# Splitting the last but one V chunk's load into three, and storing 48 rows instead of 128, in a one-core decode block

## The chip, the cores and the metric

The kernel runs on one core of one Trainium2 chip. The metric is the device time of one execution in microseconds (us). A core has five engines that work side by side and meet only at semaphores: PE (matmuls, with its weight loads shown as PEld), DVE and ACT (elementwise work), POOL (constants here) and SP (here it does nothing but issue transfers). The data of a transfer is moved by 16 DMA engines, which all work on the same transfer, each on some of its rows.

## The reference

One decode step: layer norm of a row `x` of 512, 32 query heads over 8 cached KV heads of 65536 keys each, the output projection, a residual, and a bilinear GLU with a second residual. Everything is float32.

```python
h  = x + A(layernorm(x))                    # A: the attention
h2 = h + B(layernorm(h))                    # B: (h Wgate * h Wup) Wdown
# A: q = (x @ wq) -> 32 heads of 128;  k_cache, v_cache: 8 heads x 65536 x 128
scores = einsum("bhqd,bhkd->bhqk", q, k) * 128 ** -0.5
p = softmax(scores);  o = einsum("bhqk,bhkd->bhqd", p, v);  return o @ wo
```

The caches are 512 MB of the 565 MB that are read; the rest is weights.

## The kernel before

The caches are cut into 64 chunks of 128 rows by 16384 columns of float32 (8 MB each): for each of the 8 heads four K chunks and then four V chunks, in the order in which they are used. Two tiles, `kv0` and `kv1`, take the even and the odd chunks in turn. SP issues every load, in a fixed order written out by hand (`even`, `odd`, a loop over the heads, and then the last loads one by one); before each load it waits for `free`, which DVE raises when PE is done with the tile's previous content. All loads stand in one queue, and the DMA engines work through it in order.

Chunk 62 is the last but one V chunk (of the last head) and the last that `even` loads. Behind it in the queue come chunk 63 in four pieces, the gate and up weights (`in_gu`) into `kv0`, the down weights (`in_wd`) into `kv1`, and at the very end the store of the result.

PE multiplies a chunk in 32 windows of 512 columns (`windows`, L365 of the profile). For an even chunk it waits for `s_k0` before window 0, for `s_k16` before 16, for `s_k24` before 24 and for `s_k28` before 28; each wait is for 16, and the amount is taken off again. A whole chunk is one load and raises only `s_k0`; so POOL puts 16 on the other three at the start for each even chunk (`sem_inc(p, w * (end // 2 + n))`, `end // 2` being 32). Only the weights `in_gu`, which come in four pieces, raise all four semaphores by themselves.

A transfer's own end is told by small packets: each DMA engine that took part writes one to the semaphore behind its data, 16 in all for a transfer of 128 rows.

At the end `pva` holds the result in two rows, 0 and 32, of 256 columns. DVE copies 64 rows of it into the tile `y` (128 by 256, set to zero at the start), SP stores the tile, and the host picks rows 0 and 32.

Of the kernel before, what the change touches and what calls it, by code (L numbers as in the profile page):

```python
# [3 lines left out]
F32 = mybir.dt.float32  # L4
# [4 lines left out]
P = 128  # L9
D = 512  # L10
HKV, REP, DH = 8, 4, 128
SK = 65536
CK = 16384
# [10 lines left out]
SIDE = 9  # L24
LATE = 1
WIDE = 384
DVE_ACT = bass.OrderedEngineSet([mybir.EngineType.DVE, mybir.EngineType.Activation])
K_CUTS = (0, 4, 8, 12, 16, 32)
V_CUTS = (0, 8, 12, 16, 24, 28, 32)
# [14 lines left out]
def body(nc, xr, kvd, wq0, wqo, wo7, gu, wd, out):  # L44
    pe_e, dve_e, act_e, pool_e, sp = nc.tensor, nc.vector, nc.scalar, nc.gpsimd, nc.sync

    def tile(name, *shape, align=32):
        return nc.alloc_sbuf_tensor(name, list(shape), F32, align_bytes=align).ap()
# [14 lines left out]
    kv = [tile(f"kv{i}", P, CK, align=1024) for i in range(2)]  # L63
# [3 lines left out]
    ln_s, ln_m, ln_v, ln_t, ln_r = (tile(n, 1, 1) for n in ("ln_s", "ln_m", "ln_v", "ln_t", "ln_r"))  # L67
    ln_w, ln_r3 = tile("ln_w", P, WIDE), tile("ln_r3", P, 1)
    ln_s3 = ln_w[:, 0:1]
# [9 lines left out]
    gu_sb, uf, y = tile("gu_sb", P, 512), tile("uf", P, 2, 2, 4, 2), tile("y", P, 256)  # L79
# [8 lines left out]
    def sem(name):  # L88
        sems.append(nc.alloc_semaphore(name))
        return sems[-1]  # L90
# [7 lines left out]
    s_k0, s_k16, s_k24, s_k28 = (sem(f"s_k{i}") for i in (0, 16, 24, 28))  # L98
    s_v0, s_v8, s_v16, s_v24, s_v28 = (sem(f"s_v{i}") for i in (0, 8, 16, 24, 28))
# [3 lines left out]
    late, s_act, s_pool, s_y, s_a, s_out = (sem(n) for n in ("late", "s_act", "s_pool", "s_y", "s_a", "s_out"))  # L103
    gu_t = kv[0].rearrange("p (k x) -> p k x", k=KT)[:, :, 0:2 * F]
    wd_t = kv[1]
    end = 2 * HKV * NT

    def take(e, s, n=1):
        e.wait_ge(s, n).then_inc(s, -n)  # L109
# [7 lines left out]
    def even(g):  # L117
        sp.dma_start(kv[0], kvd[g]).then_inc(s_k0, 16)

    def odd(g):  # L120
# [11 lines left out]
        out=ident, in_=ident, compare_op=ALU.not_equal, fill=1.0, base=0,  # L132
        pattern=[[-1, P]], channel_multiplier=1))
    pool.tick(pool_e.memset(qx, 0.0))
    for p, w, n in ((s_k16, 16, 0), (s_k24, 16, 0), (s_k28, 16, 0), (s_v8, 17, 0),
                    (s_v16, 16, -1), (s_v24, 16, -1), (s_v28, 16, -1)):
        pool_e.sem_inc(p, w * (end // 2 + n))
    for t in (o_pad, f_pad, sel_pad, acc, y, ln_w):
# [16 lines left out]
    take(sp, wf)  # L155
    sp.dma_start(wo_sb, wo7).then_inc(s_w, 16)
    take(sp, free)
    even(end - 2)
    take(sp, free)
    for lo, hi, p in ((0, 16, s_v0), (16, 24, s_v16), (24, 28, s_v24), (28, 32, s_v28)):  # L160
        cs = slice(lo * 512, hi * 512)
# [11 lines left out]
    for c in range(SIDE, NC):  # L173
# [13 lines left out]
        out=ln_m, in0=ln_s, scalar1=1.0 / D, scalar2=None, op0=ALU.mult))  # L187
    mine(dve_e.tensor_scalar(
        out=xd, in0=x_row, scalar1=ln_m[:, 0:1], scalar2=None, op0=ALU.subtract))
    dve_e.scalar_tensor_tensor(  # L190
        out=xs, in0=xd, scalar=1.0, in1=xd, op0=ALU.mult, op1=ALU.mult,
# [5 lines left out]
        out=xn_row, in0=xd, scalar1=ln_r[:, 0:1], scalar2=None, op0=ALU.mult).then_inc(dt, 1)  # L197
    dve_e.tensor_reduce(
        out=sel_h, in_=ident.rearrange("p (g h) -> p h g", h=REP), axis=AX.X, op=ALU.add).then_inc(own, 1)
# [4 lines left out]
        out=neg_mean, in0=mean_m, scalar1=sel_1[:, 0:1], scalar2=-1.0, op0=ALU.mult,  # L204
# [9 lines left out]
    qd = qx.rearrange("p (j x) -> p j x", j=4)  # L214
    with nc.Fori(0, HKV, engines=DVE_ACT):
        for s in range(NT):
# [20 lines left out]
        for s in range(NT):  # L237
# [12 lines left out]
            out=mrow, in_=sm[1][0:1, 0:P].rearrange("p (g h) -> p h g", h=REP), axis=AX.X,  # L250
# [5 lines left out]
            out=nbias, in0=sm[0][:, 0:1], scalar1=-SCALE, scalar2=None, op0=ALU.mult).then_inc(da, 1)  # L256
        for n in range(NT):
# [8 lines left out]
            if n == NT - 1:  # L266
                mine(dve_e.tensor_reduce(out=l1, in_=sums, axis=AX.X, op=ALU.add))
                dve_e.tensor_scalar(
                    out=l4, in0=sel_h, scalar1=l1[:, 0:1], scalar2=None, op0=ALU.mult).then_inc(tok, 1)
# [7 lines left out]
            else:  # L277
                for cs in (slice(0, 256), slice(256, 512)):
                    dve_e.tensor_tensor(  # L279
                        out=orow[:, cs], in0=ps[1][:, cs], in1=orow[:, cs], op=ALU.add).then_inc(tob, 1)  # L280
# [7 lines left out]
        for half, p in ((0, tok), (1, s_a)):  # L288
            cs = slice(half * 256, half * 256 + 256)
            dve_e.scalar_tensor_tensor(  # L290
                out=acc[:, cs], in0=attn[:, cs], scalar=1.0, in1=acc[:, cs], op0=ALU.mult, op1=ALU.add,
# [8 lines left out]
        out=acol, in_=ptp[1].rearrange("p (k j x) -> p k j x", k=KT, j=4)[:, :, :, 0], axis=AX.X,  # L300
# [4 lines left out]
    def centred(o, a):  # L305
# [8 lines left out]
        out=ln_q2, in0=hn, scalar=1.0, in1=hn, op0=ALU.mult, op1=ALU.mult,  # L314
        accum_out=ln_s3))
    dve_e.tensor_scalar(
        out=ln_s3, in0=ln_s3, scalar1=KT * EPS, scalar2=None, op0=ALU.add).then_inc(tl, 1)
    take(dve_e, kd)
    for half in range(2):
        cs = slice(half * 256, half * 256 + 256)  # L320
# [6 lines left out]
        out=sj[:, 0:2, :], in0=gux[0][:, :, :, 0], in1=uf[:, 0, :, :, 1], op=ALU.mult).then_inc(qt, 1)  # L327
# [4 lines left out]
        out=sj[:, 2, :], in0=gux[1][:, 0, :, 0], in1=uf[:, 1, 0, :, 1], op=ALU.mult)  # L332
    for o, g, u in ((f_pad[:, 0:1, 0], gux[0][:, 0, 3:4, 0], uf[:, 0, 1, 3:4, 0]),
# [3 lines left out]
            out=o, in0=g, scalar=ln_r3[:, 0:1], in1=u, op0=ALU.mult, op1=ALU.mult)  # L337
    i.then_inc(s_v8, 1)
    take(dve_e, kd)
    for half in range(2):  # L340
        cs = slice(half * 256, half * 256 + 256)
        dve_e.scalar_tensor_tensor(
            out=res[:, cs], in0=ps[1][:, cs], scalar=ln_r3[:, 0:1], in1=acc[:, cs],
# [37 lines left out]
    def step():  # L381
        pe_e.wait_ge(tl, next(once))
# [40 lines left out]
    step()  # L423
    mm(sm[0][:, 0:WIDE], mean_m, ln_w, start=True, stop=True).then_inc(pd, 1)
    for half in range(2):
# [64 lines left out]
    dve_e.tensor_copy(y[0:64, :], pva[0:64, 0:256]).then_inc(s_y, 1)  # L490
    take(sp, s_pool)
    sp.wait_ge(s_y, 1)
    sp.dma_start(out, y).then_inc(s_out, 16)
    nums = [s.num for s in sems]
    assert s_out.num == max(nums)
    sp.sem_clear(range(min(nums), s_out.num))
# [43 lines left out]
```

## Time and profile before

| What | Value |
|---|---|
| Median of 3 runs (lowest to highest) | 1309.93 us (1309.9 to 1310.06) |
| The profiled execution's own time | 1309.89 us |
| Its span, first to last instruction | 1308.5 us |
| Read from memory, over the span | 564.66 MB, 432 GB/s |
| Busy: PE, DVE, ACT | 52%, 9%, 4% of the span |
| DMA queue of SP | 99.8% of what 16 DMA engines have in time |

The profile is of one execution. The busy shares tell how long an engine worked, not whether anyone waited for it; that is read from the waits and from the chain of work that ended last. The DMA view can be asked for any stretch of the span: it then counts the packets that started in it, with their size classes, and the time that they took as a share of what 16 engines would have. The packets under 512 B are the semaphore packets.

### The profile page before, as it was taken

Reading aid. Unit: us, or ns where it says so; the run is one execution under the profiler, and the core shown is the slowest. Engines: PE = TensorE matmul, PEld = TensorE weight load, DVE = VectorE, ACT = ScalarE, POOL = GpSimd, SP = SyncE. Lnnn points to the kernel's source line nnn. Section 1 sums busy time; section 2 is a strip of 40 time slices with the busy share of each in tenths; the row PEclk is TensorE's granted clock in tenths of the full one; section 3 lists DMA queues with packets and bytes.
Section 4 is the critical chain, followed back from the end, with each engine's and each line's share of the span. In section 5 each row is a group of like instructions: output and inputs, shape, how many; then the busy total and the mean of one; then the engine's idle time right before and its main releaser. Section 6 shows DMA issues by size and latency. Waiting matters only on the chain. (4 is left out here: it accounts for less than half of the span.)

```text
span 1308.5 us, 10829 instructions
## 1 busy us (share of the span) xinstructions
PE 680.3 (52%) x4608; PEld 190.5 (15%) x4608; DVE 111.5 (9%) x286; ACT 54.9 (4%) x106; POOL 3.1 (0%) x13
## 2 busy tenths in 40 slices
PE   4355374454654545563554636535465445545466
PEld 1011111111111111111111111101111111111122
DVE  1000010100101001000010101001010010100101
ACT  0000000000000000000000000000000000000000
POOL 0000000000000000000000000000000000000000
PEclk8777786776867768767787767777687677886679
DMA  9999999999999999999999999999999999999998
GB/s 417 417 447 437 431 447 419 447 419 447 419 447 419 447 431 437 445 421 447 419 447 419 447 419 447 431 437 445 421 447 419 447 416 450 419 447 429 437 420 371
DMA packets 12931, 564.81 MB, mean 432 GB/s; under 512 B 1409, under 2 KB 1537, under 8 KB 2690
## 3 DMA queue, kind: packets, MB, share of 16 engines
q1 hardware_dynamic: 12928, 564.79, 99.8%
q8 instruction: 1, 0.02, 0.0%
q10 hardware_dynamic: 2, 0.00, 0.0%
HBM read 564.66 MB, written 0.13 MB: 432 GB/s over the span
## 5 line engine op out<-in xcount | busy, mean ns | idle before, releaser
L365 PE MATMUL ps<-kv,st 128*32 128x512 f32 x4184 | 584.2, 720 | 541.5 <-DMA kv<-in_kv 527.0
L365 PEld LDWEIGHTS ps<-kv,st 128*32 128x32 f32 x4184 | 145.1, 130 | 963.6 <-DMA kv<-in_kv 579.2
L244 DVE TENSOR_REDUCE mx<-sc 128x1 f32<-128x512 f32 x32 | 21.9, 686 | 538.0 <-DVEq L109 538.0
L415 PE MATMUL ptp<-ident,ex 128*128 128x128 f32 x128 | 27.9, 380 | 19.8 <-ACT ex L222 19.5
L218 ACT COPY sc<-ps 128x512 f32<-128x512 f32 x32 | 18.8, 586 | 451.1 <-ACTq L109 451.0
L276 DVE TENSOR_TENSOR orow<-ps,orow 128x512 f32<-128x512 f32 x16 | 11.1, 692 | 299.5 <-DVEq L109 299.5
L222 ACT ACTIVATE ex<-sc,nbias 128x512 f32<-128x512 f32 x32 | 22.8, 714 | 304.3 <-ACTq L109 304.3
L394 PE MATMUL ptp<-wqo_sb,xn 128*1 128x512 f32 x64 | 31.3, 636 | 6.4 <-DVE acc L290 5.0
L218 ACT ACT_TABLE_LOAD x8 | 10.3, 1283 | 436.3 <-ACTq L109 436.3
L263 DVE COPY st<-ptp 128x512 f32<-128x512 f32 x32 | 22.1, 692 | 44.9 <-DVEq L109 44.9
L415 PEld LDWEIGHTS ptp<-ident,ex 128*128 128x128 f32 x128 | 20.8, 193 | 22.7 <-ACT ex L222 22.6
L408 PE MATMUL sm<-ident,m 128*1 128x128 f32 x16 | 4.4, 276 | 27.2 <-DVE m L246 17.6
L279 DVE TENSOR_TENSOR orow<-ps,orow 128x256 f32<-128x256 f32 x16 | 6.0, 419 | 128.5 <-DVEq L109 128.5
L274 DVE COPY orow<-ps 128x512 f32<-128x512 f32 x8 | 5.5, 692 | 98.8 <-DVEq L109 98.8
L461 PE MATMUL attn<-wqo_sb,o_pad 128*32 128x512 f32 x64 | 8.5, 605 | 5.9 <-DVE o_pad L286 5.9
L410 PE MATMUL sm<-ones,mexp 1*128 1x1 f32 x32 | 6.9, 281 | 6.7 <-DVE mexp L253 6.7
L394 PEld LDWEIGHTS ptp<-wqo_sb,xn 128*1 128x1 f32 x64 | 5.0, 87 | 31.7 <-issue 18.9
L226 DVE COPY qrow<-ptp 1x512 f32<-1x512 f32 x8 | 5.4, 679 | 30.6 <-DVEq L109 30.6
L457 PE MATMUL ptp<-ident,orow 128*128 128x128 f32 x32 | 6.1, 300 | 3.0 <-DVE orow L279 3.0
L408 PEld LDWEIGHTS sm<-ident,m 128*1 128x1 f32 x16 | 1.3, 79 | 41.8 <-DVE m L246 24.9
L290 DVE SCALAR_TENSOR_TENSOR acc<-attn,acc 128x256 f32<-128x256 f32 x16 | 6.2, 422 | 10.8 <-DVEq L109 10.8
L398 PE MATMUL sm<-ident,qrow 1*128 1x1 f32 x32 | 3.2, 201 | 7.1 <-DVE qrow L226 7.1
(83 smaller groups left out, 78.0 us busy)
## 6 DMA issues: line engine op xcount, KB each, us to landing
wqo_sb<-in_wqo SPq DMA_DIRECT2D x7, 2048.0 KB, 32.7
kv<-in_kv SPq DMA_DIRECT2D x1, 4096.0 KB, 21.6
kv<-in_gu SPq DMA_DIRECT2D x1, 3584.0 KB, 18.8
kv<-in_kv SPq DMA_DIRECT2D x1, 2048.0 KB, 26.1
kv<-in_kv SPq DMA_DIRECT2D x2, 1024.0 KB, 29.1
kv<-in_gu SPq DMA_DIRECT2D x1, 1792.0 KB, 22.6
kv<-in_wd SPq DMA_DIRECT2D x1, 1536.0 KB, 19.3
kv<-in_wd SPq DMA_DIRECT2D x5, 256.0 KB, 20.9
```

The lines of the kernel that those rows point to most:

```text
L218: act_e.copy(sc[s], ps[s % 2]).then_inc(ad, 1)
L222: act_e.activation(ex[s - n], sc[s], AF.Exp, bias=nbias[:, 0:1], scale=SCALE, accum_out=sums[:, s:s + 1]).then_inc(atok[s - n], 1)
L244: dve_e.tensor_reduce(out=mx[:, s:s + 1], in_=sc[s], axis=AX.X, op=ALU.max).then_inc(own, 1)
L263: dve_e.tensor_copy(st[:, :, 0:16].rearrange("p g (b h) -> p b g h", h=REP), ptp[n % 2].rearrange("p (b g h) -> p b g h", b=4, h=REP)).the ...
L276: mine(dve_e.tensor_tensor(out=orow, in0=ps[n % 2], in1=orow, op=ALU.add))
L290: dve_e.scalar_tensor_tensor(out=acc[:, cs], in0=attn[:, cs], scalar=1.0, in1=acc[:, cs], op0=ALU.mult, op1=ALU.add, accum_out=rsum[:, hal ...
L365: i = mm(ps[buf][32 * j:32 * j + 32, :], st[:, 8 * j + r, :], kv[buf][:, w * 512:(w + 1) * 512], start=(r == 0), stop=(r in (2, 3, 7)), sk ...
L394: i = mm(ptp[0][0:1, :], xn[:, k:k + 1], wq_sb[:, k, :], start=(k == 0), stop=(k == KT - 1))
L410: mm(sm[0][:, 0:1], mexp.rearrange("p g h -> p (g h)"), ones[0:1, 0:1], start=True, stop=True).then_inc(pd, 1)
L415: i = pe_e.transpose(ptp[half][:, b * P:(b + 1) * P], ex[half][:, b * P:(b + 1) * P], ident)
L457: i = pe_e.transpose(ptp[1][:, b * P:(b + 1) * P], orow[:, b * P:(b + 1) * P], ident)
L461: i = mm(attn[32 * r:32 * r + 32, :], o_pad[:, r, :], wo_sb[:, r, :], start=True, stop=True)
```

## The change

Three things are edited.

1. SP loads chunk 62 in three transfers instead of one: columns 0 to 15487 of all 128 rows (raises `s_k0`), columns 15488 to 16383 (`SHARE`, 896 of them) of rows 0 to 119 (raises `s_k24`), and the same columns of rows 120 to 127 (raises `s_k28`).
2. POOL puts on `s_k24` and `s_k28` 16 less at the start, since chunk 62 raises them now by its own transfers.
3. The result's tensor has 48 rows instead of 128, and the store takes 48 rows of `y`; rows 0 and 32 are among them.

```diff
+SHARE = 896
...
-    for p, w, n in ((s_k16, 16, 0), (s_k24, 16, 0), (s_k28, 16, 0), (s_v8, 17, 0),
+    for p, w, n in ((s_k16, 16, 0), (s_k24, 16, -1), (s_k28, 16, -1), (s_v8, 17, 0),
                     (s_v16, 16, -1), (s_v24, 16, -1), (s_v28, 16, -1)):
         pool_e.sem_inc(p, w * (end // 2 + n))
...
-    even(end - 2)
+    for rows, cs, p in ((slice(0, P), slice(0, CK - SHARE), s_k0), (slice(0, 120), slice(CK - SHARE, CK), s_k24),
+                        (slice(120, P), slice(CK - SHARE, CK), s_k28)):
+        sp.dma_start(kv[0][rows, cs], kvd[end - 2][rows, cs]).then_inc(p, 16)
...
-    sp.dma_start(out, y).then_inc(s_out, 16)
+    sp.dma_start(out, y[0:48, :]).then_inc(s_out, 16)
...
-    out = nc.dram_tensor("out_y", (P, 256), F32, kind="ExternalOutput").ap()
+    out = nc.dram_tensor("out_y", (48, 256), F32, kind="ExternalOutput").ap()
```

The only engine whose queue changes is SP. Before, these rows stand there around chunk 62 (each row is a source line, the transfer, and the tile's shape):

```order
L156 DMA wqo_sb<-in_wo 128x2048
L118 DMA kv<-in_kv 128x16384
L162 DMA kv<-in_kv 128x8192
L162 DMA kv<-in_kv 128x4096
L162 DMA kv<-in_kv 128x2048 x2
L165 DMA kv<-in_gu 128x2x3584
```

After, the lines of the source are three or so further down, and the same place reads:

```order
L157 DMA wqo_sb<-in_wo 128x2048
L161 DMA kv<-in_kv 128x15488
L161 DMA kv<-in_kv 120x896
L161 DMA kv<-in_kv 8x896
L165 DMA kv<-in_kv 128x8192
L165 DMA kv<-in_kv 128x4096
L165 DMA kv<-in_kv 128x2048 x2
L168 DMA kv<-in_gu 128x2x3584
```

One transfer of 128 by 16384 became three; everything behind them stands in the same order as before.

More of the change, by code (lines that the diff above doesn't have):

```diff
@@ L535 @@
     ]
-    out = nc.dram_tensor("out_y", (P, 256), F32, kind="ExternalOutput").ap()
+    out = nc.dram_tensor("out_y", (48, 256), F32, kind="ExternalOutput").ap()
     body(nc, *args, out)
     r = run_bass_kernel_spmd(nc, [{f"in_{n}": a for n, a in arrays.items()}], core_ids=[0])
-    return np.asarray(r.results[0]["out_y"])[0:64:32].reshape(1, 1, D)
+    return np.asarray(r.results[0]["out_y"])[0:48:32].reshape(1, 1, D)
```

## The prediction

> **What bounds the kernel now.** I read the page first: who is busy all the time.
>
> ```profile
> span 1308.5 us, 10829 instructions
> PE 680.3 (52%) x4608; PEld 190.5 (15%) x4608; DVE 111.5 (9%) x286; ACT 54.9 (4%) x106; POOL 3.1 (0%) x13
> DMA packets 12931, 564.81 MB, mean 432 GB/s; under 512 B 1409, under 2 KB 1537, under 8 KB 2690
> q1 hardware_dynamic: 12928, 564.79, 99.8%
> q8 instruction: 1, 0.02, 0.0%
> q10 hardware_dynamic: 2, 0.00, 0.0%
> ```
>
> Queue q1 holds everything that SP issues, and its packets fill 99.8% of the time of 16 DMA engines; no compute engine passes 52%. So one DMA engine moves 564.79 MB / (16 x 0.998 x 1308.5 us) = 27.0 bytes per ns. The waits say the same from PE's side, and the chain that ended last says it for the end:
>
> ```profile
> PEld ps L365 <- DMA kv<-in_kv: 579.2, 66, 13.1
> 1281.31 19.26 DMA kv<-in_wd
> 1300.61 2.94 PE ps L365 x24
> 1305.46 0.88 PE pva L375 x8
> 1306.36 0.42 DVE y L490
> ```
>
> PE waited 66 times for a chunk, 579.2 us in all, and the chain runs through the weights' transfer to 1300.57 and then through the short rest. What matters is thus not PE's work but when each transfer's last byte is there. A transfer is done when the slowest of the 16 engines is done. So I asked the DMA view for the short stretches in which the semaphore packets (under 512 B) of one transfer fall. First chunk 0 (24.2 to 24.7), then the stretch 33.9 to 34.5, then chunk 1 (43.6 to 43.95, and 45.0 to 45.2), then chunk 62 (1258.6 to 1259.1, and 1260.0 to 1260.1), and the last 1.02 us of all loads (1304.34 to 1305.36), which has two lines:
>
> ```profile
> DMA packets 32, 1.05 MB, mean 2097 GB/s; under 512 B 16, under 2 KB 16, under 8 KB 16
> ...
> q1 hardware_dynamic: 15, 0.98, 378.9%
> q8 instruction: 1, 0.02, 9.7%
> ...
> DMA packets 30, 0.98 MB, mean 2809 GB/s; under 512 B 15, under 2 KB 15, under 8 KB 15
> DMA packets 2, 0.07 MB, mean 328 GB/s; under 512 B 1, under 2 KB 1, under 8 KB 1
> ...
> DMA packets 30, 0.49 MB, mean 983 GB/s; under 512 B 15, under 2 KB 15, under 8 KB 15
> DMA packets 7, 0.20 MB, mean 1966 GB/s; under 512 B 1, under 2 KB 1, under 8 KB 1
> ...
> DMA packets 14, 0.02 MB, mean 24 GB/s; under 512 B 2, under 2 KB 2, under 8 KB 14
> q1 hardware_dynamic: 14, 0.02, 6.3%
> ```
>
> This is the point of the whole case. Chunk 0 ends on all 16 engines within 0.5 us. At 34 us one packet of the instruction queue (0.02 MB, 9.7% of 16 engines x 0.6 us = 0.93 us) goes through one engine, while the other 15 start their next data packet. From chunk 1 on, 15 semaphore packets come together and the sixteenth alone, over 1 us later; chunk 62 still shows the same, and in the last 1.02 us of the loads only 6.3% of the DMA time is used, which is one engine in 16. So one engine fell behind once, never caught up, since all have equal work and no pause, and the whole program ends about 1.02 us later than 15 of its 16 engines would allow.
>
> **The change, part by part.** *Who carries what.* The page counts 1409 packets under 512 B: 16 for each of SP's 88 transfers (63 whole chunks, 4 pieces of one, 20 of weights, the store: 1408), and one for the single row `x` on q10, whose two packets are a data packet and a semaphore packet. So 128 rows go in 16 equal shares of 8 whole rows, and 1 row goes in one share, to one engine. Read on, 120 rows make 15 shares of 8, and the 8 rows 8 shares of 1. No transfer of this trace has either shape. On this reading, of the last 896 columns one engine carries nothing, seven carry 8 rows as before, and eight carry 9.
>
> [...]
>
> *The spared engine.* It moves 8 rows x 896 x 4 bytes = 28,672 bytes less, at 27.0 bytes per ns 1.06 us. If it is the late one, it is 1.02 - 1.06 = 0.04 us ahead of the others.
>
> *The other fifteen.* Their 8 rows of 3584 bytes are packets of their own now instead of the ends of longer ones. The nearest price is the 2 KB packets of the fence above: 6.3% x 16 x 1.02 us for 12 of them and 2 semaphore packets is 84 ns each, against 2048 / 27.0 = 76; so 8 ns for a packet, 0.07 us for eight. The eight engines with a ninth row add 3584 / 27.0 + 8 = 141 ns. So the last of the fifteen is later by 0.07 us (if it has no ninth row) to 0.21 us. I take the middle, 0.14. From below, nothing speaks for a gain here.
>
> Gain of the split: 1.02 - 0.14 = 0.88 us (0.81 to 0.95).
>
> *Does the end see it?* The rows from the timeline around the places that could hide it:
>
> ```profile
> 1228.50 0.34 SPq L118 DMA_DIRECT2D kv<-in_kv  x1
> 1248.40 1.75 SPq L162 DMA_DIRECT2D kv<-in_kv  x4
> 1260.42 8.80 PE L365 MATMUL ps<-kv,st 128*32 128x512 f32 x64 [7.44 <-DMA kv<-in_kv]
> 1271.32 5.55 PE L365 MATMUL ps<-kv,st 128*32 128x512 f32 x48 [2.10 <-PEq L109]
> 1279.87 1.06 PE L365 MATMUL ps<-kv,st 128*32 128x512 f32 x8 [1.37 <-DMA kv<-in_kv]
> 1288.36 7.81 PE L365 MATMUL ps<-kv,st 128*32 128x512 f32 x56 [2.55 <-DMA kv<-in_gu]
> 1300.61 2.94 PE L365 MATMUL ps<-kv,st 128*32 128x512 f32 x24 [1.15 <-DMA kv<-in_wd]
> ```
>
> SP's two more issues cost some 0.44 us each (four took 1.75). They follow 1228.50, and SP's next issue waits for `free` until 1248.40: hidden, and nobody waits behind them. PE's wait for chunk 62 ends at 1260.42; its first 15488 columns are there 1.06 us earlier, since the late engine's share of them is shorter by that. The two small loads are needed only at window 28 of 32, some 7.7 us into PE's 8.80, and land within 0.3 us of the first: hidden. Chunk 63 starts at 1271.32 not on a transfer but on its weights `st`, which follow from the end of chunk 62 and so move too; its last part again waits for the transfer (1.37 us of idle before 1279.87), as do `in_gu` (2.55) and `in_wd` (1.15). Each of these transfers stands behind chunk 62 in a queue without gaps, so all of them land 0.88 us earlier, and the waits that end last are the same as before. What is late next is the eight engines with a ninth row, by some 0.2 us.
>
> POOL's smaller amounts are the same number of instructions: nothing. PE's waits on `s_k24` and `s_k28` are there before too.
>
> *The store.* Rows of it, from the DMA view of 1307.6 to 1308.2 and from the timeline and the issues:
>
> ```profile
> DMA packets 144, 0.13 MB, mean 219 GB/s; under 512 B 16, under 2 KB 144, under 8 KB 144
> q1 hardware_dynamic: 144, 0.13, 65.5%
> 1306.81 0.34 SPq L493 DMA_DIRECT2D out_y<-y  x1
> out_y<-y SPq DMA_DIRECT2D x1, 128.0 KB, 1.7
> ```
>
> 128 data packets and 16 semaphore packets take 65.5% x 0.6 us = 0.39 us on each engine: 8 rows at about 48 ns. With 48 rows each engine has 3, since 16 divides 48: 5 x 48 = 0.24 us less. Nothing covers the store; it is the end of the program. The bounds are 0 (if the 1.7 us from issue to landing are all latency) and 0.39 (if it were all packets). I take 0.24.
>
> Sum: -0.88 - 0.24 = -1.12 us on the profiled 1309.89, so 1308.77. The median of the runs is 0.04 above that execution; 1308.8.
>
> **The rivals.**
>
> *The late engine is not the one spared.* For the forecast speaks that the lag (1.02 us) is what one engine carries of those 896 columns (1.06), but that is no evidence on which engine it is; I find no row that names it. Then it keeps its lag and gets 0.07 to 0.21 us on top: 1309.93 + 0.14 - 0.24 = 1309.83 (1309.75 to 1309.9). The same comes out if the change does not do what it says, because 120 rows are spread over all 16 engines anyhow. [...]
>
> *Slower: 120 rows go to few engines.* If the split takes 8 engines with 15 rows each, those eight carry 15 x 141 ns = 2.11 us instead of 1.06, and one more row from the last transfer: +1.19 us. If the late engine is one of the eight, the end is 1.19 later and the store gives 0.24 back: 1310.9. It is slower than before as soon as the late engine's extra passes the store's 0.24 us, that is from two more rows on. Against it: the 128 rows are in as many shares as there are engines.
>
> *The lag is not there without the profiler, or a second instruction packet falls behind chunk 62.* The profiled time equals the median within 0.04, which speaks against the first. A second packet would cost the 0.93 us of the first and cancel the gain: 1309.7. The page has one such packet in 1308 us.
>
> **How the numbers follow.** 0.2% of this time is 2.6 us, about what a measurement of this kernel can tell from no change, and none of the cases reaches it. The forecast has 0.70 (its own range 1308.5 to 1309.1: the split 0.81 to 0.95, the store 0 to 0.39), the late engine not spared 0.18, few engines 0.06, a second packet 0.03, and 0.03 for what I have not seen. The range holds the first two: from 1308.4 to 1310.0. Faster by over 0.2% would need a second gain larger than the first: 0.02; slower by over 0.2% would need a load that stalls for 2.6 us: 0.03; within 0.2%: 0.95.
>
> **What the new profile would show.** Packets 12931 + 71 = 13002 (chunk 62 adds 128 data and 23 semaphore packets, the store loses 80), 1432 of them under 512 B. The semaphore packets of the loads behind chunk 62 come within 0.5 us of each other, 16 together; the stretch with one busy engine at the end is gone. The store lands about 1.45 us after its issue. If the sixteenth packet still comes alone, the spared engine was another, and the prediction is wrong by the split's 0.88 us; if eight come late together, the rows went to few engines.

## The result, and the profile after

The changed kernel takes 1311.91 us (median of 22 runs, 1311.64 to 1312.35) against 1309.95 for the kernel before: a ratio of 1.0015, 95% interval 1.0009 to 1.0022. It is 1.96 us slower; the forecast was 1.1 us less, in a range from 1308.4 to 1310.0. From its page, with the same lines as before:

```profile
span 1310.4 us, 10831 instructions
PE 685.5 (52%) x4608; PEld 191.5 (15%) x4608; DVE 111.9 (9%) x286; ACT 54.9 (4%) x106; POOL 3.1 (0%) x13
DMA packets 13002, 564.73 MB, mean 431 GB/s; under 512 B 1432, under 2 KB 1480, under 8 KB 2761
q1 hardware_dynamic: 12999, 564.71, 99.7%
```

The packets are those that were counted beforehand, 13002 and 1432: 120 rows do make 15 shares and 8 rows 8. The DMA engines are as busy as before and move less, 431 GB/s. The chain that ended last has the same links:

```profile
1283.31 19.23 DMA kv<-in_wd
1302.58 2.95 PE ps L368 x24
1308.36 0.42 DVE y L493
```

The transfer of the weights `in_wd` is waited for until 1302.54 instead of 1300.57, and everything behind it is as long as it was, within 0.03 us. So the loss lies ahead of that point, in the queue. Where, a stretch by stretch view tells; here DMA's packets from 1257.9 to 1262.9, the time of the split columns, in the kernel before and in the changed one:

```profile
DMA packets 79, 2.06 MB, mean 413 GB/s; under 512 B 16, under 2 KB 16, under 8 KB 16
DMA packets 169, 1.77 MB, mean 355 GB/s; under 512 B 24, under 2 KB 24, under 8 KB 126
```

A stretch counts packets by their start, so such a sum is rough. Spread over each packet's own time (the trace has the start and the duration of each), the means are 433 and 301 GB/s: 0.66 MB are missing, about 1.5 us of the rate before, and the rate is under 300 GB/s for three of these microseconds. Inside, from 1258.0 to 1259.05, only short packets start in the changed kernel (rows of 3584 bytes):

```profile
DMA packets 64, 0.23 MB, mean 218 GB/s; under 512 B 0, under 2 KB 0, under 8 KB 64
q1 hardware_dynamic: 64, 0.23, 94.3%
```

94.3% x 16 x 1.05 us for 64 packets is 248 ns each, where the prediction reckoned with 141. The engines are busy, at about half their rate. Over all 128 short packets the mean is 215 ns by their own times; the first, which start when few others have, take 140.

The loss does not end with the short rows. Behind them in the queue stands the first piece of chunk 63, in packets of 32 KB. Of these, with their semaphore packets, fifteen start from 1258.6 to 1259.1 in the kernel before and nine from 1259.45 to 1259.75 in the changed one. The last line is all that starts in the changed kernel from 1259.95 to 1261.2:

```profile
q1 hardware_dynamic: 30, 0.49, 229.1%
q1 hardware_dynamic: 18, 0.29, 351.1%
DMA packets 5, 0.02 MB, mean 14 GB/s; under 512 B 0, under 2 KB 0, under 8 KB 5
```

By share x 16 x stretch, less 9 ns for each semaphore packet, a packet of 32 KB takes 1.21 us before and 1.86 after. By the packets' own times all 128 take 1.213 us before; after, the first 16 take 1.93 on average and the next 16 take 1.39. The five short packets of the last line come one after another from one engine, the late one. So while it alone still has short rows (its last ends at 1261.71), the other fifteen are in whole 32 KB rows and are slow as well.

### The profile page after: what moved, and what is told of

Same layout as the page of the kernel before. It is cut to its first block, busy times and chain, and to the rows that moved or that the text cites. A ratio compares the mean times of both kernels' runs of the same rounds, so it can differ in the third digit from the quotient of the medians.

```text
span 1310.4 us, 10831 instructions
## 1 busy us (share of the span) xinstructions
PE 685.5 (52%) x4608; PEld 191.5 (15%) x4608; DVE 111.9 (9%) x286; ACT 54.9 (4%) x106; POOL 3.1 (0%) x13
## 2 busy tenths in 40 slices
DMA packets 13002, 564.73 MB, mean 431 GB/s; under 512 B 1432, under 2 KB 1480, under 8 KB 2761
## 5 line engine op out<-in xcount | busy, mean ns | idle before, releaser
L368 PE MATMUL ps<-kv,st 128*32 128x512 f32 x4184 | 590.4, 727 | 538.3 <-DMA kv<-in_kv 523.8
## 6 DMA issues: line engine op xcount, KB each, us to landing
kv<-in_kv SPq DMA_DIRECT2D x2, 1024.0 KB, 31.9
```

The source lines that it names most:

```text
L368: i = mm(ps[buf][32 * j:32 * j + 32, :], st[:, 8 * j + r, :], kv[buf][:, w * 512:(w + 1) * 512], start=(r == 0), stop=(r in (2, 3, 7)), sk ...
```

## The experiments

My theory after this: with 120 rows, or 8, the engines are dealt the rows in such a way that two of them at a time write to one part of the tile and slow each other there (crowding); no run had shown this yet. Rivals: short rows that lie 64 KB apart are slow by themselves; each more transfer costs a pause; the store is the cause.

**The two edits apart, and all rows in one load.** First the store alone: the kernel before with

```diff
-    sp.dma_start(out, y).then_inc(s_out, 16)
+    sp.dma_start(out, y[0:48, :]).then_inc(s_out, 16)
```

> The store of 48 rows alone, chunk 62 in one load as before. Every theory of the split expects the same here: the loads as before, and the store shorter by 5 packets of 48 ns, so 0.24 us under the kernel before (1309.7), with the store landing about 1.45 us after its issue instead of 1.70. If the store were the cause of the loss, this kernel would be about 2 us slower than before.

Measured: 1309.87 against 1310.0 us, ratio 1.0 (0.9991 to 1.0009). In its trace the store lands 2.77 us after the last load's landing, in the kernel before 2.87. The store is not the cause. What it saves is 0.10 us, not 0.24; in the other traces too a store of 48 rows lands 2.75 to 2.83 us after the last load.

Then the changed kernel with the store of 128 rows:

> The three loads of chunk 62 alone, the store of 128 rows as before. If the split is the whole cause: 0.24 us above the changed kernel, 1312.15, and the DMA rate falls to about 60% for some 4 us after 1258 as in the changed kernel. If the store had a part in the loss, it is nearer to 1310.

Measured: 1311.84 us, ratio 1.0016 (1.0006 to 1.0025). That is 1.84 us over the kernel before, so within the runs' scatter the split is the whole loss; the 0.24 us expected on top of the changed kernel do not show.

Then the changed kernel with the same 896 columns as one load of all 128 rows:

```diff
-(slice(0, 120), slice(CK - SHARE, CK), s_k24), (slice(120, P), slice(CK - SHARE, CK), s_k28)
+(slice(0, P), slice(CK - SHARE, CK), s_k24)
```

> Chunk 62 in two loads: 15488 columns of all 128 rows, then the 896 columns of all 128 rows in one transfer; store of 48 rows. Crowding theory (the uneven row counts put the rows on the engines in such a way that two engines at a time write to the same part of the tile): nothing is uneven here, each 3584-byte packet takes the 140 ns that it took at first in the changed kernel, no dip of the rate; 8 x 7 ns more than the store alone, so 1309.75. Short-row theory (rows of 3584 bytes that lie 64 KB apart are read slowly, whatever the row count): the packets take 250 to 320 ns as in the changed kernel, and it ends at 1311 or later. Break theory (each more transfer in the queue costs a pause): half the loss of the changed kernel, about 1310.8.

Measured: 1309.95 us, ratio 0.9999 (0.999 to 1.0009). From 1258.2 to 1258.6 only its short and semaphore packets start:

```profile
DMA packets 50, 0.15 MB, mean 385 GB/s; under 512 B 7, under 2 KB 7, under 8 KB 50
q1 hardware_dynamic: 50, 0.15, 95.0%
```

95.0% x 16 x 0.4 us, less 7 semaphore packets of 9 ns, is 140 ns for each of 43. The same bytes, in rows of the same length from the same places, run at full rate when all 128 rows stand in one transfer. The short-row theory falls, and so does the break theory: the median is 0.08 us from that of the store alone, less than the runs scatter.

**Transfers measured by themselves, and the late engine's place.** Thirteen loads at the start, each awaited, and seven tiny ones behind chunk 62 (k rows of 8 * k columns; the waits and the two loads from the weights are left out here):

```diff
+    for rows, w in PROBES:
+        sp.dma_start(pt[rows, 0:w], last[rows, CK - w:CK]).then_inc(s_p, 16)
...
+    for k in range(9, 16):
+        sp.dma_start(pt[0:k, 128 * (k - 9):128 * (k - 9) + 8 * k], kvd[end - 2][0:k, 0:8 * k]).then_inc(s_q, 16)
```

> A kernel for measuring transfers by themselves: the kernel before, with 13 extra loads into a spare tile at its start, each awaited before the next is issued, so its total is some 60 us longer. In order: 896 columns of 128 rows, of 120, of the last 8; 2048 columns of 128 rows, 120, the first 64, the last 64, the first 112, the last 8, the 8 rows 0, 4, 8 to 28, the first 8; then 2048 columns from a weight tensor whose rows lie 8 KB apart, 128 rows and 120. Crowding theory: 128 rows run at 27 bytes per ns and engine (3584 bytes: 140 ns, 8192 bytes: 310 ns a packet); 120, 112 and 64 rows show packets that take about twice as long once the first have been taken in, from the weight tensor too; the 8 neighbouring rows take some 4 times 310 ns to land, the 8 rows that are 4 apart do not. Short-row theory: 3584-byte rows are slow also for 128 rows, 8192-byte rows are not slow for any count, and the weight tensor is never slow. Also, directly behind chunk 62, seven tiny loads of 9, 10, up to 15 rows (one row to an engine): the late engine's packet comes 1 us after the others in those of them that it takes part in, and so its place among the 16 is counted. If it were the last of the 16, as the prediction had it, none of the seven would show a late packet; the changed kernel's trace, in which the late engine carried 8 short rows and no ninth, says that it is one of the places 8 to 14 (counted from 0), so 1 to 7 of them do.

Rows of 8 KB: the stretches with 128 rows and with 120 rows, and then the same two from the weight tensor, whose rows lie 8 KB apart (stretches of 5, 6, 4.5 and 6.5 us):

```profile
q1 hardware_dynamic: 144, 1.05, 59.8%
q1 hardware_dynamic: 135, 0.98, 71.2%
q1 hardware_dynamic: 144, 1.05, 64.5%
q1 hardware_dynamic: 135, 0.98, 62.7%
```

The share times 16 times the stretch gives 48 us of packets for 128 rows and 68 for 120, then 46 and 65: fewer rows take longer, wherever in memory they lie. By the packets' own times the median is 309 ns for 128 rows and 600 for 120, 568 and 537 for the two halves of 64 rows. The expectation missed in three places. 3584-byte rows of 120 alone had a median of only 150 ns; why, no run shows. 112 rows had 416 ns, 1.3 times the 309 instead of about twice. And 8 neighbouring rows of 8 KB (522 ns for the last 8, 416 for the first 8) were hardly slower than 8 that are 4 apart (418); the next probe takes longer rows.

The tiny loads: one stretch (1317.4 to 1317.7, 0.9 us and more after the other engines' packets of the seven) holds five data packets and their five semaphore packets, beside 13 packets of the next load:

```profile
DMA packets 23, 0.43 MB, mean 1427 GB/s; under 512 B 10, under 2 KB 10, under 8 KB 10
```

By their sizes (352 to 480 bytes) they are those of the loads of 11 to 15 rows; 9 and 10 rows have no late one. So, if a load of k rows goes to the first k places, the late engine is the eleventh, place 10 counted from 0. In the changed kernel's own trace the load of 120 rows has 15 landings, the last of them 2.2 us after the fourteenth, and the load of 8 rows has none so late: there, by the same count, the late engine is one of the places 8 to 14. The 120 rows went to places 0 to 14 by it: the split spared place 15, which was in time.

**Which side is crowded.** Loads of whole 64 KB rows at the start, eleven pairs of tile rows and memory rows:

```diff
+    for i, (to, frm) in enumerate(PROBES):
+        sp.dma_start(kv[0][to, :], kvd[end - 2][frm, :]).then_inc(s_p, 16)
+        sp.wait_ge(s_p, 16 * (i + 1))
```

> The kernel before with 11 loads of whole 64 KB rows into tile kv0 at its start, each awaited before the next (the tile is loaded anew afterwards). In order, 8 rows (one to each of 8 engines): to tile rows 0 to 7; the same rows of memory to tile rows 0, 4, .. 28; the same to 0, 16, .. 112; rows 0, 16, .. 112 of memory to tile rows 0, 16, .. 112; these to 0, 4, .. 28; rows 120 to 127 to the same. Then 16 rows: to tile rows 0 to 15; to 0, 4, .. 60; to 0, 8, .. 120. Then 120 rows, then 128. Write-side crowding: only the rows of the tile matter, and a packet of 64 KB that takes 2.42 us alone takes a multiple of it where engines meet; tile rows 0, 4, .. 28 should take 2.4 to 2.5 us wherever in memory they come from, and neighbouring tile rows several times that. Read-side rival: 8 neighbouring rows of memory are slow wherever they go, rows 16 apart are fast. Count rival: only the number of engines matters, all 8-row loads take the same. [...]

One row of the DMA view for six of the loads, lines 1, 2, 3, 5, 10 and 11 of the table below:

```profile
q1 hardware_dynamic: 16, 0.52, 37.6%
q1 hardware_dynamic: 16, 0.52, 29.5%
q1 hardware_dynamic: 16, 0.52, 31.9%
q1 hardware_dynamic: 16, 0.52, 31.5%
q1 hardware_dynamic: 135, 7.86, 88.1%
q1 hardware_dynamic: 144, 8.39, 91.1%
```

Share x 16 x stretch / number of data packets is the mean time of a 64 KB row:

| Tile rows | Memory rows | Stretch, us | Share | us a row |
|---|---|---|---|---|
| 0 to 7 | 0 to 7 | 11 | 37.6% | 8.3 |
| 0, 4, .. 28 | 0 to 7 | 5 | 29.5% | 3.0 |
| 0, 16, .. 112 | 0 to 7 | 7 | 31.9% | 4.5 |
| 0, 16, .. 112 | 0, 16, .. 112 | 8 | 29.9% | 4.8 |
| 0, 4, .. 28 | 0, 16, .. 112 | 5 | 31.5% | 3.2 |
| 120 to 127 | 120 to 127 | 11 | 38.6% | 8.5 |
| 0 to 15 | 0 to 15 | 12 | 72.2% | 8.7 |
| 0, 4, .. 60 | 0 to 15 | 8 | 60.9% | 4.9 |
| 0, 8, .. 120 | 0 to 15 | 7 | 67.1% | 4.7 |
| 0 to 119 | 0 to 119 | 43 | 88.1% | 5.1 |
| 0 to 127 | 0 to 127 | 22 | 91.1% | 2.5 |

Lines 1 to 3 read the same memory and differ by up to 2.8 times; lines 2 and 5, and lines 3 and 4, read other memory and agree within 7%. It is the rows of the tile that count: the crowding is on the write side, and the read-side and the count rival fall. In units of the 2.42 us that a 64 KB row of a whole chunk takes in the kernel before, 8 or 16 neighbouring rows take 3.4 to 3.6, rows 4 apart 1.2 to 1.3 in a load of 8 and 2.0 in one of 16, and rows 8 or 16 apart 1.85 to 2.0. Rows of 64 KB in a load of 120 run at 5.1 us each, half the rate of those in a load of 128, at 2.5. What the engines share at such rows of the tile, no run shows.

**Parts and sizes of the split.** The columns as 64 and 64 rows, so that the engines have equal work:

```diff
-(slice(0, 120), slice(CK - SHARE, CK), s_k24), (slice(120, P), slice(CK - SHARE, CK), s_k28)
+(slice(0, 64), slice(CK - SHARE, CK), s_k24), (slice(64, P), slice(CK - SHARE, CK), s_k28)
```

> The 896 columns of chunk 62 as rows 0 to 63 and rows 64 to 127 instead of 120 and 8, everything else as in the changed kernel: 16 engines carry 4 rows in each of the two loads, so nobody is spared and nobody has more. Crowding theory: 64 neighbouring rows ran at 540 to 570 ns for 8 KB in the separate measurement instead of 309, so 8 short rows at some 250 ns instead of 140: the DMA rate dips for 1 to 2 us and the end is 0.9 to 1.5 us later than with all rows in one load (1309.95), near 1311.1. Rival, unequal work is what costs (15 engines, then 8): no loss here, 1310.0.

Measured: 1311.83 us, ratio 1.0014 (1.0005 to 1.0024). Equal work does not help, so it is not the uneven work that costs. The loss is larger than I expected, 1.88 us over the load of all rows instead of 1.2.

The changed kernel without its third load, and without its second:

> The changed kernel without its third load: the 896 columns of rows 120 to 127 are left out (the tile keeps there what chunk 60 left). Crowding theory, with the 120 rows as the cause: still slow, 1311.4 to 1311.8, and the dip of the rate is there. [...]

> The changed kernel without its second load: the 896 columns of rows 0 to 119 are left out, so every engine is spared 1.06 us and eight of them carry one short row. Crowding theory: the 8 rows cost little, the whole stream ends 0.9 to 1.06 us earlier than the kernel that stores 48 rows (1309.87), 1308.8 to 1309.0, and the late engine stays 1 us behind the others. If the 8 neighbouring rows are what costs, the end is at 1309.3 or later.

Measured: 1311.64 us, ratio 1.0013 (1.0003 to 1.0023), and 1308.99 us, ratio 0.9993 (0.9983 to 1.0003). Of the 1.96 us the last 8 rows carry about 0.27 (1311.91 - 1311.64, medians whose runs scatter by 0.6 to 0.7), the 120 rows the rest. Without the 120 rows every engine has 1.06 us less, and the end is 0.88 us earlier than with the store alone (1309.87), with no run above 1309.29, where the kernel before in the same series has none under 1309.72: the end does follow the bytes that are left out, as the prediction had it.

Twice the columns:

```diff
-SHARE = 896
+SHARE = 1792
```

> The split with 1792 columns instead of 896. Crowding theory: the loss grows with the bytes that go the crowded way, so from 2.0 us to about 3.5 to 4 us, 1313.4 to 1313.9, with twice as long a dip. Rival, a fixed cost of two more transfers of uneven shape: as the changed kernel, 1311.9. The prediction's own reckoning, without crowding, would have it at about 1310.2 (fifteen engines as before, eight with 0.27 us more).

Measured: 1314.19 us, ratio 1.0034 (1.0021 to 1.0046): 4.26 us over the 1309.93 of the kernel before in the same series, where 896 columns cost 1.96, and more than the 3.5 to 4 expected. A fixed cost is out. Its stretch from 1257.9 to 1262.9 is all at half rate:

```profile
DMA packets 116, 1.13 MB, mean 226 GB/s; under 512 B 23, under 2 KB 23, under 8 KB 98
```

226 GB/s, against 413 in the kernel before by the same count.

**The right engine spared, and a still smaller store.** With 448 columns as 100, 20 and 8 rows, places 10 to 15 should, by the same count, carry nothing of them:

```diff
-SHARE = 896
+SHARE = 448
...
+(slice(0, 100), ..., s_k16), (slice(100, 120), ..., s_k24), (slice(120, P), ..., s_k28)
```

> The late engine is the one at place 10, counted from 0 (the first probe). Here it is really spared: the last 448 columns of chunk 62 come as 100, 20 and 8 rows, which by the counts found go to engines 0 to 9 (twice) and 0 to 7; places 10 to 15 carry nothing of them, 0.53 us less each, places 0 to 9 carry 12 or 13 rows of 1792 bytes instead of 8, 0.27 to 0.33 us more, and some 0.08 us for packets. Store of 48 rows. If sparing the right engine is enough: the end moves by about -0.4 us against the store alone (1309.87), so 1309.5. Crowding theory with ten engines as crowded as fifteen: these 12 to 13 rows take twice their time, 0.85 us more, and slow the others meanwhile: 1310.3 to 1310.8.

Measured: 1310.87 us median of 12 runs, ratio 1.0018 (1.0006 to 1.0029); but the runs lie in three groups (five at 1309.74 to 1310.03, three at 1310.87 to 1311.03, four at 1315.2 to 1315.9), and the profile is of one in the first, at 1309.87. There the lag is gone: the sixteenth landing of the last load comes 0.13 us after the fifteenth instead of 1.02. But the first fifteen are now spread over 1.08 us instead of 0.31, so the end stays where it was. Sparing the right engine took the lag away, and the others lost as much: by their additional rows (0.27 to 0.33 us in the expectation's count), and because the first 16 of the next load's 32 KB packets again take 1.64 us on average instead of 1.213. What the slower groups are is open; no profile shows one.

The store of 16 rows, chunk 62 in one load:

> The kernel before with a store of 16 rows (0, 4, .. 60) instead of 128, chunk 62 in one load. The store of 48 rows landed 0.10 us sooner than that of 128 (2.77 against 2.87 us after the last load's landing, in the profiles) instead of the 0.24 that the packets' count gave. If the rest is latency that no count changes: another 0.04 us at most, 1309.8. If the packets' time counts in full: 2 packets of 48 ns less, 1309.77. Nothing speaks for slower. This is the version meant to beat both.

Measured: 1310.06 against 1309.94 us, ratio 1.0001 (0.9992 to 1.001); the store lands 2.94 us after the last load. No gain is left there. No version that I ran and that loads all of the data beats the kernel before by more than its runs scatter; nearest is the store of 48 rows alone.

## Why the prediction was wrong

- *What bounds the kernel, and the lag of one engine:* right. The end moved with the landing of the last loads (chain: +1.97 us), and the store came behind it as before. That the instruction packet makes the lag was argued from its time alone; the two probes show it. There the packet comes at 94 and at 176 us, and the sixteenth landing of the chunk before it lags the fifteenth by 0.18 and 0.16 us, that of the chunk behind it by 1.13 and 1.15.
- *Who carries what:* right in the counts (15 and 8 shares), wrong in the supposition that decided the sign of the gain. The forecast rested on the late engine being the one spared, the last of the 16, with a chance of 0.70 though "I find no row that names it". By the tiny loads it is place 10, which kept its 8 rows; with places 10 to 15 left out, as far as that count goes, the lag fell from 1.02 to 0.13 us.
- *The other fifteen:* this is the step that failed most. I priced their 8 short rows at the full rate plus 8 ns a packet, from packets of loads of 128 rows, and gave 0.07 to 0.21 us as bounds. In the place of 141 ns they took 215 on average and 248 in the middle of the stretch, and with what followed the split cost 1.96 us over the same columns in one load (1311.91 against 1309.95). The price was right for loads of 128 rows (140 ns in the load of all rows), and it had the wrong dealing of rows: every load of SP in the trace was of 128 rows, and the packets that I took it from were those of one engine that ran alone. An upper bound from a load of another row count was not to be had there, and I should have said that none excluded half the rate.
- *What stands behind it in the queue:* I had all of it land 0.88 us earlier at an unchanged rate. The first two rounds of chunk 63's 32 KB packets were slow too (1.93 and 1.39 us instead of 1.213), which no term of the sum had.
- *Does the end see it:* right in the result; the additional issues cost nothing that can be seen, nor do the waits for the two small loads. They stand at windows 24 and 28, not at 28 alone as I wrote, and the small loads land up to 2.0 us behind the first, not within 0.3. Wrong on the way: I had the first 15488 columns there 1.06 us earlier, and PE starts on them 0.33 us later than the 1260.42 of before, since the late engine's last long row takes 3.25 us there instead of 2.29:

```profile
1260.75 9.55 PE L368 MATMUL ps<-kv,st 128*32 128x512 f32 x64 [9.20 <-DMA kv<-in_kv]
```

- *The store:* right in kind, 0.10 us instead of 0.24.
- *The rivals:* "not the one spared" was true, but its 1309.83 left the crowding out too; it is near what the load of all rows shows (1309.95), where the short packets took 140 ns. The slower rival had the sign, for the wrong reason: 120 rows did go to 15 engines.
- *The chances:* 0.95 for staying within 0.2% held by luck: a loss of 0.15% came where a gain of 0.09% was forecast. The runs could tell more than I thought: the ratio's interval is 0.0007 wide on either side, not 0.002.

How 1.96 us comes from a piece of 1.06 us can be added up from the packets' own times, for the late engine, which the end follows. Its last long row of chunk 62, moved beside the crowded rows of the others, takes 3.25 us instead of the 2.29 of the load of all rows: 0.96 more. Its eight short rows take 1.81 us instead of 1.06: 0.75 more, though by then it is the only one with short rows. Its first 32 KB row takes 1.51 us instead of 1.21: 0.30 more. Together that is 2.01, and its last landing came 2.00 us later (1305.64 to 1307.64). The mean of the sixteen landings moved by 1.53 us (1304.51 to 1306.04). So by these times the lag that the split was to take away made the split dearer: the late engine is slowed beside the others' crowded rows, and the others are slow beside its own. No run has the 896 columns split without a late engine in them.

One thing stays open: why engines that move rows of a load of all 128 rows are slow (1.8 to 2.3 us for 32 KB instead of 1.213) while others move crowded ones. Two engines at one part of the tile do not explain that for all of them, and no run tried it by itself.

## What to carry to other kernels

A load's price was not its bytes alone here: rows 0 to 127 in one transfer ran at full rate (309 ns for 8 KB, 2.5 us for 64 KB), and every other count of neighbouring rows that was tried with rows of 8 KB or more ran slower: 112 rows at three quarters of the rate (416 ns for 8 KB), 120 and 64 at about half (537 to 600 ns), 8 and 16 rows of 64 KB at under a third (8.3 to 8.7 us). What stood behind the 120 rows in the queue waited, and its first 16 packets of 32 KB were slow as well (1.93 us on average instead of 1.213). Before shifting work off a late engine, find out which one it is; tiny loads of growing row counts, queued behind a large one, did that here in a single run (those of 11 to 15 rows had a late packet, those of 9 and 10 none). And where a price comes only from rows of one shape, let the range reach to what another shape could cost.

## What the runs showed of the hardware

- One 16 KB instruction packet (0.93 us long, at 34 to 36 us, in the two probes at 94 and 176) put one DMA engine about 1 us behind: its landing of the chunk behind the packet lagged the fifteenth by 1.13 and 1.15 us in the two probes. It stayed so to the last load, some 1270 us later (1.02 us in the kernel before, 1.28 in the changed one), except where the split with 448 columns spared it (0.13 us).
- A 64 KB row took 2.5 to 8.7 us on average, by where in the tile the other rows of its transfer go; where it came from in memory made at most 7% in the pairs tried.
- While rows of the 120-row load were still being moved, at the last by one engine alone, the 32 KB packets of the other engines took 1.8 to 2.3 us each. Behind the load of all rows, which had a late engine too, all took 1.213.
- A store's 128 rows of 1 KB landed 0.10 us later than 48 rows, though the packets add up to 0.24 us more an engine, and 16 rows (every fourth one) were no faster than 48 (2.94 against 2.77 us after the last load).
